# Loading q and k of the first four groups four tokens to a partition, one half of the heads on each partition half

## The chip, the cores and the metric

The kernel runs on one core of one Trainium2 chip. The metric is the device time of one execution in microseconds, the median of the timed runs. A profiled execution gives the span, the engines' records and the granted TensorE clock. A run is called slow when it is over 1.5% above the fastest of the same kernel.

## The reference

Attention over 4 batches, 8 heads, 768 tokens and 64 channels per head, with 4 sink tokens and a window of 128, then a feed-forward layer (512 to 2048, exact GELU, 2048 to 512) on all 3072 tokens.

```python
scores = scale * np.matmul(q, k.transpose(0, 1, 3, 2))
keep = is_sink | in_window                 # rel = query - key in 0..127, or key < 4
scores = np.where(keep, scores, -1e9)
a = softmax(scores)
attn = np.matmul(a, v)
x = attn.transpose(0, 2, 1, 3).reshape(B * S, H * D)
h = x @ w_in
g = 0.5 * h * (1.0 + erf(h / np.sqrt(2)))
out = g @ w_out                            # float32
```

The inputs q, k and v are 0.1 times normal numbers, so the scores are close to zero and the softmax is nearly flat. The comparison does not vouch for the order of q and k.

## The kernel before

The tokens are cut into twelve groups of 256. Everything that the first 60 us need comes through one load queue in a fixed order, into ten staging buffers:

```python
STREAM = [
    ("q", 0), ("k", 0), ("v", 0), ("q", 1), ("k", 1), ("wi", 0), ("wi", 1), ("v", 1), ("wi", 2),
    ("wi", 3), ("wi", 4), ("wi", 5), ("wi", 6), ("wi", 7), ("k", 2), ("wo", 1), ("q", 2),
    ("wo", 2), ("wo", 0), ("v", 2), ("q", 3), ("wo", 3), ("k", 3), ("wo", 4), ("wo", 5),
    ("wo", 6), ("wo", 7), ("v", 3),
]
# then q, k, v of groups 4 to 11
```

`wi` and `wo` are eighths of the two weight matrices. Each item is 512 KB. "q3" below means the q of group 3, and so on. A load of q or k has two tokens to a partition, 128 partitions, 512 bytes in one piece:

```python
def pump(limit=None):
    ...
        st = stage.tile([P, 1024], FP32, name="st", tag="st")
        if kind in SRC:
            ...
            nc.sync.dma_start(
                out=st[:, 0:w].rearrange("p (h c) -> p h c", c=2 * D),
                in_=src.rearrange("h (p r) d -> p h (r d)", r=2),
            )
```

`take` casts an item to bf16 on the engines that a hand-made list of operations names. Then q and k are transposed on TensorE, and one or two engines copy the result out of PSUM:

```python
def qk_transpose(g, w, *engs, pt=None, pairs=(0, NPAIR)):
    ...
    for p in range(*pairs):
        for r in range(2):
            nc.tensor.transpose(
                pt[:, :, p, r * HP : (r + 1) * HP] if w else pt[:, r, p, :],
                ..., ident)
    ...
    for o, eng in enumerate(engs or (nc.vector,)):
        ps = slice(pairs[0] + o * n, pairs[0] + (o + 1) * n)
        copy(eng, dst[:, :, ps], pt[:, :, ps])
```

Scores, exponentials, masks and output products of groups 0 to 3 are woven with the products of the feed-forward layer. From about 60 us on, groups 4 to 11 run in a steady pattern that the change does not touch.

The softmax here doesn't subtract the row's maximum and nothing guards it: scores larger than these inputs give would overflow.

Of the kernel before, what the change touches and what calls it, by code (L numbers as in the profile page):

```python
# [12 lines left out]
BF16 = mybir.dt.bfloat16  # L13
# [61 lines left out]
def kernel(  # L75
# [11 lines left out]
    nc = tc.nc  # L87
    P = nc.NUM_PARTITIONS

    B, H, S, D = q.shape  # L90
# [11 lines left out]
    NPAIR = H // 2  # L102
    NKT = DM // P
    NFT = DFF // P
    NBP = S // (2 * P)
# [130 lines left out]
    def pump(limit=None):  # L236

        while head[0] < (limit or len(stream)):
            n = head[0]
            if n >= NST and not freed[n - NST]:  # L240
                return
            kind, j, *half = stream[n]
            st = stage.tile([P, 1024], FP32, name="st", tag="st")
            if kind in SRC:
                b, i = divmod(j, NBP)
                hs = slice(half[0] * H // 2, (half[0] + 1) * H // 2) if half else slice(0, H)
                src = SRC[kind][b, hs, i * Q2 : (i + 1) * Q2, :]
                w = src.shape[0] * 2 * D
                nc.sync.dma_start(  # L249
                    out=st[:, 0:w].rearrange("p (h c) -> p h c", c=2 * D),  # L250
                    in_=src.rearrange("h (p r) d -> p h (r d)", r=2),
                )
            elif kind == "wi":
                nc.sync.dma_start(  # L254
                    out=st.rearrange("p (t f) -> p t f", f=FW),
                    in_=moe_w_in[:, ts(j // 2, FW)].rearrange("(t p) f -> p t f", p=P)[
                        :, 2 * (j % 2) : 2 * (j % 2) + 2, :
                    ],
                )
            else:  # L260
                nc.sync.dma_start(
                    out=st.rearrange("p (f c) -> p f c", c=DM),
                    in_=moe_w_out[j * NW * P : (j + 1) * NW * P, :].rearrange(
                        "(f p) c -> p f c", p=P
                    ),
                )
            staged[stream[n]] = st
            head[0] += 1
# [6 lines left out]

    def take(item, *engs):

        kind, j, *half = item
        st = staged.pop(item)
        eng = engs[0]  # L280
        if kind == "wi":
# [15 lines left out]
                        src[HP * e : HP * (e + 1), r, :, :],  # L297
                    )
        else:

            n = NPAIR // 2 if half else NPAIR
            o = half[0] * n if half else 0
            if (kind, j) not in cast:
                if kind == "q":
                    cast[kind, j] = c16p.tile([P, 2, H, D], BF16, name="q16")
                else:
                    cast[kind, j] = c16p.tile([P, NPAIR, 2, 2, D], BF16, name="k16")
            t = cast[kind, j]
            if kind == "q":
                dst = t[:, :, 2 * o : 2 * (o + n), :].rearrange("p r h d -> p h r d")  # L310
                src = st[:, 0 : n * 4 * D].rearrange("p (h r d) -> p h r d", r=2, d=D)
            else:
                dst = t[:, o : o + n].rearrange("p a r h d -> p a h r d")
                src = st[:, 0 : n * 4 * D].rearrange("p (a h r d) -> p a h r d", h=2, r=2, d=D)
            n = dst.shape[1] // len(engs)
            for o, eng in enumerate(engs):
                copy(eng, dst[:, o * n : (o + 1) * n], src[:, o * n : (o + 1) * n])
# [36 lines left out]
        QKT["k", g] = qktp.tile([P, 2, NPAIR, 2, HP], BF16, name="kt")  # L354
        return QKT["k", g]

    def qk_transpose(g, w, *engs, pt=None, pairs=(0, NPAIR)):


        src = cast["qk"[w], g]  # L360
        if pt is None:
            pt = psB.tile([P, 2, NPAIR, P], BF16, name="qkps", tag="bank")
        for p in range(*pairs):
            for r in range(2):
                nc.tensor.transpose(
                    pt[:, :, p, r * HP : (r + 1) * HP] if w else pt[:, r, p, :],
                    src[:, p, r, :, :].rearrange("s h d -> s (h d)") if w else src[:, r, 2 * p : 2 * p + 2, :].rearrange("s h d -> s (h d)"),
                    ident,
                )
        if ("qk"[w], g) not in QKT:  # L370
            (k_tile if w else q_tile)(g)
        dst = QKT["qk"[w], g].rearrange("k e p r s -> k e p (r s)") if w else QKT["qk"[w], g]
        n = (pairs[1] - pairs[0]) // max(1, len(engs))
        for o, eng in enumerate(engs or (nc.vector,)):
            ps = slice(pairs[0] + o * n, pairs[0] + (o + 1) * n)
            copy(eng, dst[:, :, ps], pt[:, :, ps])

    def big16():

# [24 lines left out]

    def warm_up(n, ps):

        for _ in range(n):
            nc.tensor.matmul(
                ps[:, 0:P], lhsT=ident, rhs=ident, start=True, stop=True, skip_group_check=True
            )  # L410

    ETS = {}

# [314 lines left out]
    def run(ops):  # L728

        pt = {}  # L730
        for op in ops:
# [5 lines left out]
            elif name == "take":  # L737
                take(tuple(args), *engs)
                pump(where["q", 6])
            elif name in ("T", "T2"):  # L740
                g, w = args[0:2]
                if name == "T2":
                    pt2 = psC.tile([P, 2, NPAIR, P], BF16, name="qkps2", tag="po2") if spare else None
                    qk_transpose(g, w, *engs, pt=pt2, pairs=(2 * args[2], 2 * args[2] + 2))
                elif len(args) > 2:
                    if g not in pt:
                        pt[g] = big16()
                    qk_transpose(g, w, *engs, pt=pt[g][:, w])
# [111 lines left out]
```

## Time and profile before

| | before |
|---|---|
| median (2 runs) | 226.98 us (226.87 to 227.09) |
| span of the profiled run | 224.7 us |
| TensorE busy | 214.5 us, 95% |
| mean granted clock | 0.999 |
| groups 0 to 3 end, second chunk's first feed-forward product starts | 59.4 us |

The page of the profile gives busy time by engine, the span in 40 slices, the queues, and the chain of work that ended last. The prediction below shows its main rows. In the views PE is TensorE, PEld its weight loads, DVE VectorE, ACT ScalarE, POOL GpSimd, and SP the engine whose queue issues the loads. First, TensorE's queue runs in order, so a wait of TensorE in the first 60 us is carried to the end unless a later wait takes it up. The row of the granted clock tells how fast TensorE may run in a slice (9 is full); before, it is 9 in all of them:

```profile
PEclk9999999999999999999999999999999999999999
```

"Landing" of a load below means the last of its sixteen completion increments in the trace.

### The profile page before, as it was taken

The page shows a single profiled execution, that of the slowest core. Times are in us where ns is not written, and L with a number is a line of the kernel's source. Part 1 is how long each engine was busy: PE and PEld are TensorE (multiplying, and loading weights), DVE is VectorE, ACT ScalarE, POOL GpSimd, SP SyncE. Part 2 cuts the span into 40 slices and gives each one's busy share as a digit, 9 for nine tenths or more (in the row PEclk, how much of TensorE's full clock was granted, in tenths as well). Part 3 has the DMA queues.
Part 4 walks back from the last instruction along what each step waited for, and adds up shares of the span by engine and source line. Part 5 has one row for each costly group of instructions (what it writes and reads, how often), then busy time and mean ns, then how long its engine had stood idle before and what let it go on. Part 6 is the DMA issues. An engine that isn't in the chain of part 4 may idle for free.

```text
span 224.7 us, 4333 instructions
## 1 busy us (share of the span) xinstructions
PE 214.5 (95%) x1742; PEld 118.4 (53%) x1762; DVE 111.0 (49%) x266; ACT 124.0 (55%) x154; POOL 51.9 (23%) x95
## 2 busy tenths in 40 slices
PE   7998999899999999999999999999999999999993
PEld 7665887455544465444455444455444465444452
DVE  4378304997690288480197580297550397100121
ACT  3677757955365974065973165963157972278000
POOL 8238726544220011320011400011400011300000
PEclk9999999999999999999999999999999999999999
DMA  6999999999396994477994487995582024500112
GB/s 168 291 351 386 344 340 325 371 284 308 118 186 112 305 282 100 96 144 148 300 250 99 93 167 166 293 217 106 107 170 39 0 51 100 126 10 0 47 47 93
DMA packets 70051, 40.12 MB, mean 179 GB/s; under 512 B 27152, under 2 KB 64272, under 8 KB 70032
## 3 DMA queue, kind: packets, MB, share of 16 engines
q1 hardware_dynamic: 67968, 34.48, 59.5%
q0 software_dynamic: 1920, 5.25, 9.6%
q8 instruction: 13, 0.21, 0.4%
q10 hardware_dynamic: 144, 0.13, 0.2%
q14 instruction: 6, 0.05, 0.1%
HBM read 27.26 MB, written 6.29 MB: 149 GB/s over the span
## 4 chain that ended last, share of the span: by engine, by line
PE 82%; DVE 4%; DMA 4%; SPq 4%; issue 2%; ACT 1%; POOL 1%
PE po L670 34%; PE big L603 29%; PE bank L537 4%; DMA st<-in_v_dram 4%; PE big L467 4%; PE big L636 3%; SPq L249 3%; PE po L636 2%; PE bank L603 2%; PE bank L517 1%; POOL vo L274 1%; SPq L254 1%; ACT et L476 1%; DVE et L484 1%; PE bank L578 1%
## 5 line engine op out<-in xcount | busy, mean ns | idle before, releaser
L670 PE MATMUL po<-WOUT,gt 128*128 128x512 bf16 (+1 forms) x380 | 86.5, 371 | 2.0 <-issue 1.6
L603 PE MATMUL big<-xt,WIN 128*128 128x512 bf16 x300 | 66.1, 379 | 0.2
L670 PEld LDWEIGHTS <-gt 128*128 128x128 bf16 x400 | 36.1, 98 | 39.1 <-issue 3.7
L622 ACT ACTIVATE gt<-big 128x1024 bf16<-128x1024 f32 (+1 forms) x32 | 30.6, 969 | 44.7 <-PE big L603 44.7
L603 PEld LDWEIGHTS <-WIN 128*128 128x128 bf16 x320 | 31.3, 98 | 37.8
L476 ACT ACTIVATE et<-big 128x1024 bf16<-128x1024 f32 (+1 forms) x48 | 43.6, 952 | 10.7 <-PE big L467 10.5
L685 POOL DMA_DIRECT2D out_dram<-osb x40 | 22.9, 578 | 111.2 <-DVE rz L555 79.8
L484 DVE TENSOR_TENSOR et<-et,mask 128x1024 bf16<-128x1024 bf16 x30 | 21.8, 731 | 32.6 <-ACT et L476 32.0
L274 DVE COPY osb<-po 128x512 f32<-128x512 f32 (+1 forms) x24 | 15.9, 665 | 37.8 <-PE po L670 29.5
L559 DVE TENSOR_TENSOR xg<-bank,rz 128x256 bf16<-128x256 f32 x44 | 18.7, 424 | 1.5
L537 PEld LDWEIGHTS <-et 128*128 128x128 bf16 x352 | 14.8, 97 | 6.6 <-issue 1.2
L274 DVE CAST vo<-st 64x512 bf16<-64x512 f32 x38 | 16.9, 443 | 1.8 <-DMA st<-in_v_dram 1.4
L467 PE MATMUL big<-qt,kt 64*128 64x128 bf16 (+1 forms) x256 | 15.6, 238 | 0.5 <-DVE kt L274 0.2
L616 ACT ACTIVATE gt<-big 128x1024 bf16<-128x1024 f32 (+1 forms) x8 | 9.8, 1238 | 11.0 <-PE big L603 11.0
L537 PE MATMUL bank<-vo,et 128*128 128x65 bf16 x326 | 14.9, 193 | 0.1
L636 PEld LDWEIGHTS <-WIN 128*128 128x128 bf16 x128 | 12.2, 98 | 1.6 <-issue 0.2
L491 DVE TENSOR_TENSOR et<-et,mask 128x768 bf16<-128x768 bf16 x14 | 7.8, 564 | 9.9 <-ACT et L476 9.5
L467 PEld LDWEIGHTS <-kt 64*128 64x128 bf16 x256 | 8.4, 94 | 7.9 <-issue 5.3
L701 ACT ACT_TABLE_LOAD x9 | 11.5, 1283 | 0.2
L555 DVE RECIPROCAL rz<-bank 128x4 f32<-128x4 f32 x44 | 7.7, 174 | 6.4 <-PE bank L537 3.9
L274 DVE CAST q<-st 128x1024 bf16<-128x1024 f32 (+1 forms) x12 | 7.6, 634 | 6.0 <-DMA st<-in_q_dram 5.8
L636 PE MATMUL big<-xt,WIN 128*128 128x256 bf16 x80 | 10.4, 272 | 0.0
(83 smaller groups left out, 146.8 us busy)
## 6 DMA issues: line engine op xcount, KB each, us to landing
st<-in_q_dram SPq DMA_DIRECT2D x12, 512.0 KB, 7.0
st<-in_k_dram SPq DMA_DIRECT2D x12, 512.0 KB, 6.7
st<-in_v_dram SPq DMA_DIRECT2D x12, 512.0 KB, 7.8
out_dram<-osb POOLq DMA_DIRECT2D x40, 128.0 KB, 2.8
st<-in_moe_w_in_dram SPq DMA_DIRECT2D x8, 512.0 KB, 9.7
st<-in_moe_w_out_dram SPq DMA_DIRECT2D x8, 512.0 KB, 8.0
out_dram<-osb SPq DMA_DIRECT2D x3, 256.0 KB, 2.0
kt<-k SPq DMA_TRANSPOSE x16, 2.8
```

The costliest lines, as they stand in the source:

```text
L274: eng.tensor_copy(out=out, in_=in_)
L467: nc.tensor.matmul(ps[:, hl, c : c + n * P], lhsT=kt(gk, p, ek, rows), rhs=qt(g, p, e, n, rows), start=not add, stop=True, skip_group_chec ...
L476: nc.scalar.activation(out=et[:, :, c0:], in_=ps[:, :, c0:], func=AF.Exp, scale=att_scale)
L484: nc.vector.tensor_tensor(out=et.rearrange("p h (e n) -> p (h e) n", e=2), in0=et.rearrange("p h (e n) -> p (h e) n", e=2), in1=mask.unsqu ...
L537: nc.tensor.matmul(pos[n][:, e * PV + hl * DV : e * PV + (hl + 1) * DV], lhsT=ets[n][:, hl, c : c + P], rhs=vo[:, h, :], start=e == 0 and ...
L559: nc.vector.tensor_tensor(out=XG[g][:, :, 2 * p : 2 * p + 2, :], in0=po[:, 0 : 2 * PV].rearrange("p (e h c) -> p e h c", e=2, h=2)[:, :, : ...
L603: nc.tensor.matmul(outs[a], lhsT=WIN[:, t, ts(f, P)], rhs=XT[c][:, :, t, :], start=(t == 0), stop=(t == NKT - 1),)
L622: nc.scalar.activation(out=gt.rearrange("k a n -> k (a n)"), in_=src, func=AF.Gelu)
L636: nc.tensor.matmul(out4[a], lhsT=WIN[:, t, ts(f, P)], rhs=XT[c][:, 2 * half : 2 * half + 2, t, :], start=(t == 0), stop=(t == NKT - 1), sk ...
L670: nc.tensor.matmul(po, lhsT=GT[c, f // 4][:, f % 4, ts(m, P)], rhs=WOUT[:, f, cols], start=(f == 0), stop=(f == NFT - 1),)
L685: nc.gpsimd.dma_start(out=out[r0 : r0 + P, :].rearrange("(s r) c -> r s c", r=2)[r], in_=osb[HP * r : HP * (r + 1), :],)
L701: nc.scalar.activation(out=warm[:, 1:2], in_=warm[:, 0:1], func=func)
```

## The change

The intent is longer packets: 1024 bytes instead of 512 for q and k of the first 1024 tokens. Four tokens go to one partition, so 256 tokens fill 64 partitions; heads 0 to 3 go to the lower half of the partitions and heads 4 to 7 to the upper half. One load becomes two of 256 KB. The transposed tokens then stand in another order in PSUM, and the copy out of PSUM puts them right by reading pairs that are 32 elements apart.

```diff
-            if kind in SRC:
+            if kind in "qk" and j < 4:
                 b, i = divmod(j, NBP)
+                for hg in range(2):
+                    nc.sync.dma_start(
+                        out=st[HP * hg : HP * (hg + 1), :].rearrange("p (h c) -> p h c", c=4 * D),
+                        in_=SRC[kind][
+                            b, hg * H // 2 : (hg + 1) * H // 2, i * Q2 : (i + 1) * Q2, :
+                        ].rearrange("h (p r) d -> p h (r d)", r=4),
+                    )
... (casts: the same elements in another order)
-        for p in range(*pairs):
-            for r in range(2):
+        for j in range(2):
+            for a in range(2):
+                for r in range(2):
+                    if w:
+                        dst = pt.rearrange("k e (g j) (r a n) -> k j r a g e n", j=2, r=2, a=2)
+                    else:
+                        dst = pt.rearrange("k r (g j) (e a n) -> k j r a g e n", j=2, e=2, a=2)
+                    nc.tensor.transpose(dst[:, j, r, a], ..., ident)
...
-            copy(eng, dst[:, :, ps], pt[:, :, ps])
+            copy(
+                eng,
+                dst[:, :, ps].rearrange("k b p (c n a) -> k b (p c) n a", c=2, a=2),
+                pt[:, :, ps].rearrange("k b p (c a n) -> k b (p c) n a", c=2, a=2),
+            )
... (warm_up: the same columns of fill matmuls, in instructions of up to 512)
```

More of the change, by code (lines that the diff above doesn't have):

```diff
@@ L241, in pump @@
                 return
-            kind, j, *half = stream[n]
+            kind, j = stream[n]
             st = stage.tile([P, 1024], FP32, name="st", tag="st")
-            if kind in SRC:
+            if kind in "qk" and j < 4:
                 b, i = divmod(j, NBP)
-                hs = slice(half[0] * H // 2, (half[0] + 1) * H // 2) if half else slice(0, H)
-                src = SRC[kind][b, hs, i * Q2 : (i + 1) * Q2, :]
-                w = src.shape[0] * 2 * D
+                for hg in range(2):
[5 more added lines that the diff above has]
+                    )
+            elif kind in SRC:
+                b, i = divmod(j, NBP)
                 nc.sync.dma_start(
-                    out=st[:, 0:w].rearrange("p (h c) -> p h c", c=2 * D),
-                    in_=src.rearrange("h (p r) d -> p h (r d)", r=2),
+                    out=st.rearrange("p (h c) -> p h c", c=2 * D),
+                    in_=SRC[kind][b, :, i * Q2 : (i + 1) * Q2, :].rearrange(
+                        "h (p r) d -> p h (r d)", r=2
+                    ),
                 )
@@ L276, in take @@
     def take(item, *engs):
-        kind, j, *half = item
+        kind, j = item
         st = staged.pop(item)
@@ L299, in take @@
         else:
-            n = NPAIR // 2 if half else NPAIR
-            o = half[0] * n if half else 0
-            if (kind, j) not in cast:
-                if kind == "q":
-                    cast[kind, j] = c16p.tile([P, 2, H, D], BF16, name="q16")
-                else:
-                    cast[kind, j] = c16p.tile([P, NPAIR, 2, 2, D], BF16, name="k16")
-            t = cast[kind, j]
-            if kind == "q":
-                dst = t[:, :, 2 * o : 2 * (o + n), :].rearrange("p r h d -> p h r d")
-                src = st[:, 0 : n * 4 * D].rearrange("p (h r d) -> p h r d", r=2, d=D)
-            else:
-                dst = t[:, o : o + n].rearrange("p a r h d -> p a h r d")
-                src = st[:, 0 : n * 4 * D].rearrange("p (a h r d) -> p a h r d", h=2, r=2, d=D)
+            if j < 4:
+                t = c16p.tile([P, 2, 4, 2, D], BF16, name=kind + "16")
+                dst = t.rearrange("p a r h d -> p a h r d")
+                src = st.rearrange("p (a h r d) -> p a h r d", h=2, r=4, d=D)
+            elif kind == "q":
+                t = c16p.tile([P, 2, H, D], BF16, name="q16")
+                dst = t.rearrange("p r h d -> p h r d")
+                src = st.rearrange("p (h r d) -> p h r d", r=2, d=D)
+            else:
+                t = c16p.tile([P, NPAIR, 2, 2, D], BF16, name="k16")
+                dst = t.rearrange("p a r h d -> p a h r d")
+                src = st.rearrange("p (a h r d) -> p a h r d", h=2, r=2, d=D)
+            cast[kind, j] = t
             n = dst.shape[1] // len(engs)
@@ L355, in k_tile, with qk_transpose @@
         return QKT["k", g]
-    def qk_transpose(g, w, *engs, pt=None, pairs=(0, NPAIR)):
+    def qk_transpose(g, w, *engs, pt=None):
         src = cast["qk"[w], g]
@@ L362, in qk_transpose @@
             pt = psB.tile([P, 2, NPAIR, P], BF16, name="qkps", tag="bank")
-        for p in range(*pairs):
-            for r in range(2):
-                nc.tensor.transpose(
-                    pt[:, :, p, r * HP : (r + 1) * HP] if w else pt[:, r, p, :],
-                    src[:, p, r, :, :].rearrange("s h d -> s (h d)") if w else src[:, r, 2 * p : 2 * p + 2, :].rearrange("s h d -> s (h d)"),
-                    ident,
-                )
-        if ("qk"[w], g) not in QKT:
-            (k_tile if w else q_tile)(g)
-        dst = QKT["qk"[w], g].rearrange("k e p r s -> k e p (r s)") if w else QKT["qk"[w], g]
-        n = (pairs[1] - pairs[0]) // max(1, len(engs))
-        for o, eng in enumerate(engs or (nc.vector,)):
-            ps = slice(pairs[0] + o * n, pairs[0] + (o + 1) * n)
-            copy(eng, dst[:, :, ps], pt[:, :, ps])
+        for j in range(2):
[5 more added lines that the diff above has]
+                        dst = pt.rearrange("k r (g j) (e a n) -> k j r a g e n", j=2, e=2, a=2)
+                    nc.tensor.transpose(
+                        dst[:, j, r, a],
+                        src[:, j, 2 * a + r].rearrange("s h d -> s (h d)"),
+                        ident,
+                    )
+        (k_tile if w else q_tile)(g)
+        dst = QKT["qk"[w], g].rearrange("k e p r s -> k e p (r s)") if w else QKT["qk"[w], g]
+        n = NPAIR // len(engs)
+        for o, eng in enumerate(engs):
+            ps = slice(o * n, (o + 1) * n)
+            copy(
+                eng,
+                dst[:, :, ps].rearrange("k b p (c n a) -> k b (p c) n a", c=2, a=2),
+                pt[:, :, ps].rearrange("k b p (c a n) -> k b (p c) n a", c=2, a=2),
+            )
     def big16():
@@ L405, in warm_up @@
     def warm_up(n, ps):
-        for _ in range(n):
+        while n > 0:
+            w = min(n, 4)
             nc.tensor.matmul(
-                ps[:, 0:P], lhsT=ident, rhs=ident, start=True, stop=True, skip_group_check=True
+                ps[:, 0 : w * P],
+                lhsT=ident,
+                rhs=ident.unsqueeze(1).to_broadcast((P, w, P)),
+                start=True,
+                stop=True,
+                skip_group_check=True,
             )
+            n -= w
     ETS = {}
@@ L739, in run @@
                 pump(where["q", 6])
-            elif name in ("T", "T2"):
+            elif name == "T":
                 g, w = args[0:2]
-                if name == "T2":
-                    pt2 = psC.tile([P, 2, NPAIR, P], BF16, name="qkps2", tag="po2") if spare else None
-                    qk_transpose(g, w, *engs, pt=pt2, pairs=(2 * args[2], 2 * args[2] + 2))
-                elif len(args) > 2:
+                if len(args) > 2:
                     if g not in pt:
```

## The prediction

> **What bounds the kernel now.** I read the page first: which engine is busy, and where it is not.
>
> ```profile
> span 224.7 us, 4333 instructions
> ...
> PE 214.5 (95%) x1742; PEld 118.4 (53%) x1762; DVE 111.0 (49%) x266; ACT 124.0 (55%) x154; POOL 51.9 (23%) x95
> ...
> PE   7998999899999999999999999999999999999993
> ...
> DMA  6999999999396994477994487995582024500112
> GB/s 168 291 351 386 344 340 325 371 284 308 118 186 112 305 282 100 96 144 148 300 250 99 93 167 166 293 217 106 107 170 39 0 51 100 126 10 0 47 47 93
> ```
>
> TensorE is busy 95% of the span. A slice is 5.6 us; slices below 9 lie in the first nine, about 50 us, and in the last. In those 50 us the DMA row stands at 9 and stays there until 58 us. So the end is set by TensorE, whose queue is in order: what is lost in the first 50 us shifts all that follows, and nothing later can win it back. The changed lines touch only this stretch (the first four groups of 256 tokens). About 10 us of TensorE idle is the most that a perfect repair could give, 4.5%; a stall of 4.5 us would be needed for a loss of 2%.
>
> Next the chain of work that ended last, in order of time, for the first 20 us: which wait ends last there?
>
> ```profile
> 1.94 1.36 SPq L249
> ...
> 3.35 1.62 SPq L249
> ...
> 5.00 1.74 SPq L249
> ...
> 9.08 9.11 DMA st<-in_v_dram
> ```
>
> Columns are start, length, what. The load queue is held up, 1.6 to 1.7 us for each 512 KB load, and the eighth load of the stream (v of group 1) lands at 18.19. GpSimd then casts it until 21.6, and the waits of TensorE show 1.0 us for that cast (at 21.70). From there TensorE runs closed up to 36 us. So the landing time of load 8 sets the start of all that follows; q0, k0, q1 and k1 lie in front of it.
>
> Rates by window (mean DMA share, then GB/s, stand last):
>
> ```profile
> 5.00:11.00 6.00, 5.52 (x75) 4.29 (x73) 2.44 (x5) 3.68 (x6) 2.20 (x6) 1.00 1.20 290
> 18.00:22.00 4.00, 3.01 (x43) 2.31 (x40) 3.12 (x7) 3.15 (x4) 3.53 (x5) 1.00 1.07 390
> ```
>
> From 5 to 11 us only q, k, v come, as 512-byte packets: 290 GB/s, 1.81 us for a load of 524288 bytes. From 18 to 22 us weights come as 2048-byte packets: 390 GB/s. The packet records give the same: 33.6 ns mean for 512 bytes, 88.6 ns for 2048. The intent of the change is plain: 1024-byte packets for q and k.
>
> A second critical place is at 37 to 47 us, where the chain passes through VectorE (0.69 us kt copy, then casts, L484, q copy), and the timeline of VectorE is closed:
>
> ```profile
> 37.64 0.69 DVE L274 COPY kt<-qkps 128x1024 bf16<-128x1024 bf16 x1 [0.19 <-PE qkps L365]
> 38.25 1.06 DVE L274 CAST WOUT<-st 128x1024 bf16<-128x1024 f32 x1
> 39.23 0.83 DVE L274 CAST q<-st 128x512 bf16<-128x512 f32 x1
> ...
> 41.56 0.69 DVE L484 TENSOR_TENSOR et<-et,mask 128x1024 bf16<-128x1024 bf16 x1
> 42.17 1.26 DVE L274 CAST k<-st 128x512 bf16<-128x512 f32 x1
> 43.35 0.68 DVE L274 COPY qt<-qkps 128x1024 bf16<-128x1024 bf16 x1
> ```
>
> No idle bracket after the second line until 44.95; TensorE waits for L484 at 42.3 and for L559 at 44.63 (0.66 us).
>
> **What the Trainium skill says.** (1) "SBUF — State Buffer", section on the DMA port swizzle: partitions 0 to 63 reach only 8 of 16 ports, as do 64 to 127; it measured 196 GB/s for 64 partitions against 328 for 128 at 1 MiB, and two loads to the two halves do not add up. The trace has the like: output stores from 64 partitions against those from 128.
>
> ```profile
> out_dram<-osb POOLq DMA_DIRECT2D x40, 128.0 KB, 2.8
> ...
> out_dram<-osb SPq DMA_DIRECT2D x3, 256.0 KB, 2.0
> ```
>
> Half the bytes take longer. In the packet records a pair of half stores (2 x 128 KB, about 188 us) takes 1.59 us, 165 GB/s, and one full 256 KB store (212.6 us) 0.80 us, 327 GB/s. The agreement is good, though queue and direction differ from a load. (2) "VectorE: DVE Perf Modes", auto-detection: two 16-bit elements per cycle out of PSUM need step 1. The trace agrees for contiguous copies: 0.68 us for 1024 elements, under the 1.07 us that one per cycle at the 0.96 GHz of that page would need. (3) "DMA: Bandwidth & Descriptors", rules: two transfers to disjoint halves serialize.
>
> **The change, part by part.**
> Loads. Each of 8 loads (512 KB, 1024 packets of 512 bytes over 128 partitions) becomes two of 256 KB, 256 packets of 1024 bytes each, on 64 partitions. The effective time of a packet is 16 engines x bytes / rate: 28.2 ns at 512 and 84 ns at 2048; a straight line between gives 46.8 ns at 1024, 350 GB/s, 1.50 us a load. That is the hoped case: 0.31 us saved on each, 1.2 us over the four loads ahead of v1. With half the ports, an estimate from the SBUF page's 8 x 27.2 GB/s is 218 GB/s, 2.41 us: 0.60 us lost on each, 2.4 us over four. The upper bound from this trace is half of 390, 195 GB/s, 2.69 us: 3.5 us over four. I choose 2.4. Group 1's k then lands near 14.9 instead of 12.4, the weights and v1 likewise 2.4 later (20.6), its cast ends near 24.0. v1 remains what TensorE waits for, so its whole stream shifts 2.4 us. The next four loads lose 2.4 more, but q2's cast is over at 32.2 and TensorE takes it at 36.1; only k3 (cast from 42.2, needed for the copy at 45.4) could cost about 0.5.
>
> Copies out of PSUM. The eight copies now read pairs 32 elements apart. On VectorE the two-per-cycle mode should go: 512 cycles more at 0.96 GHz, 0.53 us for 1024 elements, 0.27 for 512. VectorE has four full ones (q1, q2, k2, q3) and three halves: 2.9 us in all. The early ones hide under the wait for v1. In the stretch of 37 to 47 us, q2 and k2 delay the chain to L484 by up to 1.0, q3's another 0.5: I put 1.2 on the path. ScalarE copies (1.01 and 0.59 us) I leave unchanged, having no view of a strided one.
>
> Casts: same elements, same runs of 64, no change. Transposes: the same 64, output runs 64 bytes long; q with runs of 128 elements and k with runs of 64 both take 219 ns now, so no change. Warm-up: 102 fill matmuls of 128 columns become 27 of mostly 512, the same columns; 12 fills now take 0.83 us, 69 ns each, so some 0.1 us per group, in a stretch that waits for loads: 0.
>
> Sum: 227.0 + 2.4 + 1.2 + 0.5, less 1.3 because some of these overlap each other and existing idle (0.66 us at 44.6): 229.8.
>
> **The rivals.** A: packets win. The two halves follow each other on the same engines; should those get out of step, some serve one half while others serve the other, and all ports work. Then v1 lands 1.2 us earlier, but TensorE reached that wait only 1.0 us before, and slower copies take 0.3 of it early and 1.2 later: 226 to 227.5. For it: 512-byte packets visibly cost; against it: the half stores at 165 GB/s, two in a row. B: loads are slow and everything is on the path: 3.5 for v1, 1.5 VectorE, 1 for k3 and the late weights: 233, over 2%. C: VectorE's copies stay fast and loads half-hidden: 228.5. D: everything hidden: 227; against it stands that the wait at 21.70 leaves no slack for a later landing.
>
> **Range and chances.** Half the ports or something near: 65%, giving 230.5 give or take 1; the packets win or cancel: 35%, 227.2 give or take 0.7. Together 229.8 with 226.5 to 232.0 as the range. Over 2% slower means above 231.5: 0.17. Over 2% faster means below 222.4, more than the early idle can give by this change: 0.01. Within: 0.82.
>
> **What would show it.** Rate in the early q and k windows: near 218 or below (right), near 350 (wrong, rival A). Landing of v1: near 20.6 against 18.2, and TensorE's wait for that cast still there near 24. VectorE copies from PSUM: 1.2 us for 1024 elements, 0.68 if I am wrong. TensorE's stretch of 36 to 48 us longer by about 1 us with waits on VectorE. After 60 us nothing should differ but the shift. What would make it wrong: engines that share out the ports well, or TensorE bound so tightly to other waits that the shift is absorbed.

## The result

| | before | after |
|---|---|---|
| median (2 runs each) | 226.98 us | 235.24 us (235.19 to 235.28) |
| ratio of the fast runs | | 1.0364, 95% interval 1.0319 to 1.0408 |
| span of the profiled run | 224.7 us | 233.6 us |
| mean granted clock | 0.999 | 0.985 |

The changed kernel is 3.6% slower, and its time is above the predicted range. Ratios in this document are the mean time of one kernel's fast runs over the mean of the other's of the same rounds, so they are not quite the ratios of the medians quoted.

The page of the changed kernel, rows that answer to those of before (busy time, TensorE and its clock by slices of 5.84 us, GB/s, loads of q and k):

```profile
span 233.6 us, 4207 instructions
...
PE 217.9 (93%) x1668; PEld 114.9 (49%) x1688; DVE 114.2 (49%) x266; ACT 123.9 (53%) x154; POOL 52.1 (22%) x95
...
PE   7688899859999999999999999999999999999993
...
PEclk9799999979999999999999999999999999999999
...
GB/s 136 237 295 365 310 240 295 249 351 220 274 187 170 112 274 290 104 90 174 147 299 209 120 108 151 232 290 114 146 133 92 3 45 94 90 45 3 45 45 91
...
st<-in_q_dram SPq DMA_DIRECT2D x8, 256.0 KB, 8.8
st<-in_k_dram SPq DMA_DIRECT2D x8, 256.0 KB, 9.7
```

The reader should see three things. The eight q and k items are now sixteen loads of 256 KB. TensorE has a hole in the ninth slice (5 tenths, 46.7 to 52.6 us), which it did not have before. The clock shows a 7 in the second and ninth slices, each where TensorE has been waiting.

The lag grows in two places. These are the shifts of the same instruction in the two traces:

| TensorE or ScalarE reaches | before, us | after, us | shift |
|---|---|---|---|
| first exponential | 9.34 | 12.89 | +3.56 |
| transposes of q2 | 36.00 | 40.20 | +4.20 |
| first output product of group 2 | 41.98 | 47.50 | +5.52 |
| transposes of k3 | 44.70 | 53.24 | +8.54 |
| first feed-forward product after group 3 | 59.42 | 68.26 | +8.84 |
| end | 225.03 | 233.86 | +8.83 |

So the lag is 3.6 us by the first exponential, grows by 4.3 more between 40 and 53 us, and does not grow after 60 us. These are lags at a point, not losses that add up: two runs described below come to the transposes of q2 1.3 us earlier (after_exact) and 3.4 us later (two_queues) than the changed kernel, and neither time differs from its time clearly. In the changed kernel the late place sets the end.

**The early place.** The changed kernel's chain of work that ended last (start, length, what):

```profile
3.57 7.08 DMA st<-in_v_dram
...
11.87 0.70 DVE kt L284
12.62 0.23 PE big L493 x2
```

The third and fourth of the first scores (L493) wait for VectorE's share of the copy of k, and that copy stands in VectorE's queue behind the cast of v0, whose load landed at 10.65 (8.68 before). Before, the first scores started at 8.95 and did not wait for VectorE at all.

**The late place.** First the chain of the kernel before, where wo3's cast had been waiting in VectorE's queue for its turn, not for its load:

```profile
40.06 0.59 DVE WOUT L274
...
41.56 0.69 DVE et L484
```

Then the same piece of the changed kernel's chain:

```profile
36.84 10.78 DMA st<-in_moe_w_out_dram
47.64 0.93 DVE WOUT L284
...
49.50 0.70 DVE et L510
50.25 0.40 PE bank L563 x4
```

And its VectorE timeline (start, busy time, what, in brackets the idle time ahead and what ended it):

```profile
42.09 1.21 DVE L284 COPY kt<-qkps 128x1024 bf16<-128x1024 bf16 x1
...
45.90 0.43 DVE L284 CAST q<-st 128x512 bf16<-128x512 f32 x1 [1.99 <-DMA st<-in_q_dram]
47.64 0.93 DVE L284 CAST WOUT<-st 128x1024 bf16<-128x1024 f32 x1 [1.32 <-DMA st<-in_moe_w_out_dram]
```

Before, wo3 landed at 38.85 and its cast came at 40.06, so it had 1.21 us to spare. Now it lands at 47.62, 8.77 later, and the cast follows at once. VectorE's queue is in order: behind that cast stand v2's casts and the mask (L510, before L484) that the output products of group 2 need. The mask is 7.94 later: 8.77, less the 1.21 to spare, plus 0.38 of longer queue. So a mask that has nothing to do with the weights is held up because the in-order engine ahead of it waits for a load of weights.

By stretches (start and end, length, busy time of PE, PEld, DVE, ACT and POOL, then clock, DMA share, GB/s):

```profile
5.00:11.00 6.00, 4.13 (x26) 2.05 (x24) 1.19 (x3) 2.64 (x4) 0.70 (x5) 0.85 1.12 235
...
48.00:50.00 2.00, 0.00 (x0) 0.00 (x0) 1.92 (x4) 0.00 (x0) 0.03 (x1) 1.00 1.04 364
50.00:52.00 2.00, 1.53 (x11) 0.97 (x13) 1.95 (x5) 1.54 (x2) 0.66 (x1) 0.53 1.07 365
```

From 5 to 11 us 235 GB/s move instead of 290. From 48 to 50 us TensorE does nothing, and after it the granted clock is 0.53.

### The profile page after: what moved, and what is told of

Same layout as the page of the kernel before. It is cut to its first block, busy times and chain, and to the rows that moved or that the text cites. A ratio compares the mean times of both kernels' runs of the same rounds, so it can differ in the third digit from the quotient of the medians.

```text
span 233.6 us, 4207 instructions
## 1 busy us (share of the span) xinstructions
PE 217.9 (93%) x1668; PEld 114.9 (49%) x1688; DVE 114.2 (49%) x266; ACT 123.9 (53%) x154; POOL 52.1 (22%) x95
## 4 chain that ended last, share of the span: by engine, by line
PE 77%; DMA 8%; DVE 7%; ACT 3%; issue 2%; SPq 2%; ACTq 0%
PE po L696 32%; PE big L629 28%; DMA st<-in_moe_w_out_dram 5%; PE bank L563 4%; PE big L493 4%; DMA st<-in_v_dram 3%; PE big L662 2%; ACT et L502 2%; PE bank L629 2%; DVE et L510 2%; SPq L249 2%; PE bank L543 1%; DVE vo L284 1%; DVE kt L284 1%; DVE et L517 1%
## 5 line engine op out<-in xcount | busy, mean ns | idle before, releaser
L510 DVE TENSOR_TENSOR et<-et,mask 128x1024 bf16<-128x1024 bf16 x30 | 22.0, 740 | 32.6 <-ACT et L502 32.0
L493 PE MATMUL big<-qt,kt 64*128 64x128 bf16 (+1 forms) x256 | 16.3, 241 | 1.4 <-DVE kt L284 1.0
L493 PEld LDWEIGHTS <-kt 64*128 64x128 bf16 x256 | 8.7, 95 | 10.3 <-issue 7.3
```

The costliest lines, as they stand in the source:

```text
L493: nc.tensor.matmul(ps[:, hl, c : c + n * P], lhsT=kt(gk, p, ek, rows), rhs=qt(g, p, e, n, rows), start=not add, stop=True, skip_group_chec ...
L510: nc.vector.tensor_tensor(out=et.rearrange("p h (e n) -> p (h e) n", e=2), in0=et.rearrange("p h (e n) -> p (h e) n", e=2), in1=mask.unsqu ...
```

## The experiments

The theory: the loads are the whole loss, since a load to half of the partitions is slow. A first rival: the strided copies on VectorE lengthen its closed stretches and make the waits. A second: the number of loads, sixteen instead of eight, is what costs. A third: the lowered clock is a cause. Three further questions came up on the way: why the late loads cost more than the early ones, why a fast form of the loads gains nothing, and what a false wait in the copies is worth.

All kernels of a call ran on one chip with the kernel before: 226.54, 226.56, 226.62 and 226.53 us median in the four calls (7 runs each). Every other kernel has 4 runs. The table gives all of them; the texts follow. The edits are shown shortened; conditions that confine them to q and k of the groups named are left out.

| run | median, us | range | ratio to before, 95% interval |
|---|---|---|---|
| half_ports | 236.54 | 234.72 to 236.9 | 1.0398 [1.0343, 1.0454] |
| by_heads | 227.36 | 226.28 to 228.5 | 1.0021 [0.9974, 1.0069] |
| copies_only | 229.34 | 228.58 to 231.23 | 1.012 [1.006, 1.018] |
| stripes | 231.93 | 230.55 to 233.62 | 1.0225 [1.0164, 1.0286] |
| groups_0_1 | 228.66 | 228.43 to 229.84 | 1.010 [1.007, 1.013] |
| groups_2_3 | 232.39 | 232.09 to 233.26 | 1.026 [1.0236, 1.0285] |
| stripes_plain | 227.17 | 226.61 to 227.92 | 1.0016 [0.9991, 1.004] |
| stripes_v_first | 231.32 | 230.29 to 231.74 | 1.020 [1.0171, 1.0229] |
| copies_exact | 227.10 | 226.84 to 227.34 | 1.002 [1.0002, 1.0038] |
| fills | 234.63 | 233.83 to 234.97 | 1.0347 [1.0321, 1.0373] |
| two_queues | 235.06 | 234.12 to 235.45 | 1.0365 [1.0331, 1.0398] |
| stripes_exact | 232.41 | 229.57 to 233.56 | 1.0212 [1.0145, 1.028] |
| group_3 | 229.78 | 229.45 to 230.62 | 1.0155 [1.0128, 1.0181] |
| adjacent_full | 229.45 | 228.47 to 230.37 | 1.0128 [1.0091, 1.0166] |
| adjacent_half | 232.45 | 231.33 to 233.0 | 1.0255 [1.0225, 1.0286] |
| after_exact | 235.44 | 233.99 to 236.48 | 1.0389 [1.0346, 1.0433] |

### half_ports: the kernel before, each q and k load in two partition halves

```diff
+ for g2 in range(2):
+     rows = slice(HP * g2, HP * (g2 + 1))
      nc.sync.dma_start(
-         out=st[:, 0:w]..., in_=src.rearrange("h (p r) d -> p h (r d)", r=2))
+         out=st[rows, 0:w]..., in_=src.rearrange("h (p r) d -> p h (r d)", r=2)[rows])
```

> The kernel before; each of the eight q and k loads of groups 0 to 3 is split into two loads by partition half (rows 0 to 63, then 64 to 127), still 512-byte packets, same places, same copies. Result correct. Theory 1 (loads that reach one partition half run at about half the rate, 225 GB/s in the changed kernel's first 14 us against 290): v of group 1 has its last packet near 18.9 us as in the changed kernel (16.3 before), the last v load near 53.9 (46.2 before), and the time rises by most of the 8.3 us: 232 to 235 us. Theory 2 (the strided copies out of PSUM carry the loss): 227 to 228.5 us.

Measured: 236.54 us, 1.5 above the range of theory 1. Packets stay at 512 bytes, transposes and copies are those of before, and the whole loss is there. Stretches of its trace, same columns:

```profile
44.00:46.00 2.00, 1.26 (x11) 0.37 (x9) 0.00 (x0) 0.95 (x3) 0.00 (x0) 1.00 1.18 192
46.00:48.00 2.00, 0.74 (x10) 0.47 (x11) 0.43 (x1) 0.38 (x1) 1.24 (x2) 1.00 1.19 184
```

The queue is busy (DMA share 1.18 and 1.19) and moves 192 and 184 GB/s, while TensorE is busy for 2.00 of the four us and VectorE for 0.43. The copies fall as the main cause.

### by_heads: the same number of loads, all partitions

```diff
+ for g2 in range(2):
+     hh = slice(g2 * H // 2, (g2 + 1) * H // 2)
-     out=st..., in_=src...
+     out=st...[:, hh], in_=src...[:, hh]
```

> Control of the number of loads: the kernel before with each of the same eight loads split into two by heads, each over all 128 partitions, 512-byte packets. Result correct. Theory 1 (partition halves): no change, 226.5 to 227.5 us. Rival (more and smaller loads cost by themselves): several us, up to 8.

Measured: 227.36 us, a ratio whose interval holds 1 and ends at 1.0069, or 1.6 us. So the number of loads is not the main cost; the second rival falls. One side effect is of use below: k0 lands at 8.47 instead of 6.86 although all partitions are used.

### copies_only: the changed kernel with the loads of before

Its output is wrong, which doesn't matter for the time.

```diff
-            if kind in "qk" and j < 4:
+            if False:
```

> The changed kernel with its q and k loads put back to one full load of 512-byte packets each; casts, transposes, strided copies and wide warm-up stay. The order of tokens and heads is wrong on purpose, so the result is wrong; times are valid. Theory 1: the copies (0.53 us more each on VectorE for 1024 elements, as the trace shows) cost 1 to 1.5 us: 227.5 to 229 us. Theory 2 (copies carry the loss): above 231 us.

Measured: 229.34 us, 2.8 over before and a little above the first theory's range. The TensorE timeline says where most of it begins:

```profile
8.86 0.28 PE L493 MATMUL big<-qt,kt 64*128 64x256 bf16 x2
10.57 0.23 PE L493 MATMUL big<-qt,kt 64*128 64x128 bf16 x2 [1.42 <-DVE kt L284]
```

The third and fourth of the first scores wait 1.42 us for VectorE. They read head pair 0, which ScalarE has copied; VectorE copies pairs 2 and 3. In the trace these matmuls wait for VectorE's semaphore. Each engine's copy writes its pairs in both 128-token blocks, which fits a tracking that takes this region for one unbroken stretch, from its first pair in block 0 to its last in block 1; the next experiment tests whether the two blocks matter. The wait guards nothing, and VectorE's copy stands behind v0's cast.

That the two parts interleave is not enough, though. The kernel before shares the copy of k in the same way, pairs 0 and 1 to ScalarE and 2 and 3 to VectorE, each in both blocks, and its four first scores run ahead of VectorE's part:

```profile
8.31 0.59 ACT L272 COPY kt<-qkps 128x512 bf16<-128x512 bf16 x1
8.96 0.34 PE L467 MATMUL big<-qt,kt 64*128 64x256 bf16 x4
9.91 0.42 DVE L274 COPY kt<-qkps 128x512 bf16<-128x512 bf16 x1
```

What is new is the longer pattern in which the same region is written. Why that brings the wait is not shown.

### copies_exact: each shared copy written block by block

As copies_only.

```diff
-            copy(eng, dst[:, :, ps]..., pt[:, :, ps]...)
+            for e in range(2):      # where two engines share the copy
+                copy(eng, dst[:, e, ps]..., pt[:, e, ps]...)
```

> The kernel with the full 512-byte loads and the strided copies (order wrong on purpose), with each copy that two engines share written as two instructions, one for each block of 128 tokens. In the kernel without this the first scores of pair 0 wait for VectorE's half of k (pairs 2 and 3), which they do not read, 1.42 us at 10.6 us, behind the cast of v; now they wait for ScalarE's half alone. If that wait is a cost of its own: the first exponential starts near 9.4 us in place of 10.8, and 228.0 to 228.8 us in place of 229.3. If the strided copies at 37 to 48 us carry all of it: 229 to 229.6 us.

Measured: 227.10 us, below what either side expected. In its timeline the same scores run in one group (the form of this kernel has the scores at L501):

```profile
8.81 0.35 PE L501 MATMUL big<-qt,kt 64*128 64x256 bf16 x4
```

So the false wait was about 2.2 us of the 2.8 (the two runs are of different calls), and the strided reads, with everything else in that kernel, cost 0.5.

### groups_0_1 and groups_2_3: the change in two groups at a time

```diff
-            if kind in "qk" and j < 4:
+            if kind in "qk" and j in NEW:      # (0, 1) or (2, 3); else as before
```

> The changed kernel with its new loads, casts, transposes and copies in groups 0 and 1 alone (tokens 0 to 511); groups 2 and 3 as before. Result correct. Theory A (the loads ahead of v of group 1 cost some 4 us, as in the changed kernel at 22 us, and the later four cost the other 4): 229.5 to 232 us. Theory B (a delay of the early part is absorbed by the waits of 36 to 48 us, so that the later loads carry nearly all): 227 to 229 us.

> The changed kernel with its new form in groups 2 and 3 alone; groups 0 and 1 as before, so v of group 1 has its last packet near 16.3 us. Result correct. Theory A: 229.5 to 232 us, and the two halves together give the 8.3 us. Theory B: 233 to 235 us.

Measured: 228.66 and 232.39 us, +2.1 and +5.8. The sum, 7.9, is about the whole loss of 8.3, so the two add up. Neither theory has both times in its ranges. What was missed is that the late two groups cost nearly three times as much as the early two. The landing of v3, the last load of this stretch, shows the same: 47.73 before, 50.29 with groups 0 and 1, 53.92 with groups 2 and 3. A split load costs 0.64 us in the early groups (2.56 over four) and 1.55 in the late ones (6.19 over four).

### group_3, adjacent_full, adjacent_half: why a late load costs more

group_3 is the change in q3 and k3 alone. The other two move the late loads: q3 and k3 come directly behind k2 and q2. adjacent_full has the loads of before, adjacent_half the changed form in groups 2 and 3.

```diff
-    ("wi", 7), ("k", 2), ("wo", 1), ("q", 2), ("wo", 2), ("wo", 0), ("v", 2), ("q", 3), ("wo", 3), ("k", 3), ...
+    ("wi", 7), ("k", 2), ("q", 2), ("q", 3), ("k", 3), ("wo", 1), ("wo", 2), ("wo", 0), ("v", 2), ("wo", 3), ...
```

> The changed kernel's loads, transposes and copies in group 3 alone (q3, k3); all else as before. What is to be read first is the landing of the last load of weights and v before 60 us, 47.73 us before, 50.29 with groups 0 and 1 (four split loads, 0.64 us each), 53.92 with groups 2 and 3 (1.55 us each). Theory M (a half load costs more when it stands between loads of weights, each one by itself): two split loads land the last v near 47.73 + 2 x 1.55 = 50.8. Theory N (the first two half loads throw the sixteen DMA engines out of step, and only a series of them costs 1.5): about 47.73 + 2 x 0.6 = 49.0. Time: M 229.5 to 231, N 227.5 to 229.

> The kernel before with its late loads in another order: k2, q2, q3, k3 stand next to each other, ahead of wo1, wo2, wo0, v2, wo3; full loads. It is the reference for the next run. The sum of the loads is the same, so the last weights (wo6) should land where they did before, 44.65 us give or take 0.5; the time may be a little longer because wo1, wo2, wo0 come 3.5 us later: 227 to 229.

> The same order with the four loads of groups 2 and 3 in the changed form (1024-byte packets, one half of the partitions each). Theory M (a half load is dear because loads of weights stand on both sides of it): next to each other only the ends mix, so four cost 0.6 to 0.8 us each and wo6 lands 2.4 to 3.2 us later than in adjacent_full; early, groups 0 and 1 have cost 0.64 each like this. Rival: the price in this stretch is 1.55 each in any order (something of the later stretch itself, as its deep queue): wo6 lands 6.2 us later than in adjacent_full. Time: M +2 to +3.5 us over adjacent_full, rival +5 to +6.

Landings in us:

| load | before | groups_2_3 | group_3 | adjacent_full | adjacent_half |
|---|---|---|---|---|---|
| wi7 | 26.33 | 28.02 | 26.20 | 26.57 | 27.95 |
| k3 | 40.57 | 47.29 | 44.43 | 33.05 | 36.69 |
| wo6 | 44.65 | 51.12 | 48.21 | 45.17 | 47.71 |
| v3 | 47.73 | 53.92 | 51.39 | 48.28 | 50.84 |

Two split loads among loads of weights (group_3) cost 3.66 us at v3, 1.83 each; theory M expected 50.8 and got 51.39, theory N's 49.0 is out. (Each landing is of one profiled run; v3 lands from 47.73 to 48.06 in before, copies_only and copies_exact, which have the same loads.) Four that stand together cost 2.54 at wo6, 0.64 each, the price of the early groups. So the late stretch as such is not dear. A split load is dear when full loads stand on both sides of it. The records of single packets fit: from 27 to 47 us the 2048-byte packets of the weights take 91 ns each on average before, and 126 ns in the changed kernel, beside half loads. Why full loads slow so much beside half ones is not shown by any run. The times followed as M said: adjacent_half is 3.0 us over adjacent_full. The order itself costs 2.9 us, since the weights come later, so the repair gains nothing: 232.45 against 232.39 for groups_2_3.

### two_queues: the upper halves of groups 0 and 1 from ScalarE's queue

```diff
-                    nc.sync.dma_start(
+                    (nc.scalar if hg and j < 2 else nc.sync).dma_start(
```

> The changed kernel with the upper-half loads of q and k of groups 0 and 1 issued from ScalarE's queue in place of the sync engine's, so that both halves can be in flight together. Result correct. If the halves then use all ports: 300 GB/s or more in the first q and k loads, k of group 0 landed near 7 us in place of 8.3, and 231 to 234 us. If loads to the two halves do not add up even so: 225 GB/s and 235 to 236 us.

Measured: 235.06 us. From 5 to 11 us the trace shows 236 GB/s against 235 in the changed kernel. Two halves on two queues do not add up to the full rate, as the Trainium skill has it in "SBUF — State Buffer", the section on two transfers to the two halves (+6% there). The run shows one thing more. v0 now lands at 12.82 instead of 10.65, the first exponential comes at 15.12 instead of 12.89 and the transposes of q2 3.4 us later than in the changed kernel, yet the time is the same: wo3 lands at 47.79 against 47.62, and TensorE waits for it.

### fills: the clock held up

```diff
-    ("T", [0,0], "A"), ("T", [0,1], "AV"), ... ("av", [2,0], "")
+    ("T", [0,0], "A"), ("warm", [28], ""), ("T", [0,1], "AV"), ... ("av", [2,0], "W44")
```

> The changed kernel with matmuls whose results nothing reads put into TensorE's two long waits: 28 blocks of 128 columns before the transposes of k of group 0, 44 before the first output product of group 2. Result correct. If the lowered clock behind those waits (granted 0.50 to 0.86 at 10 to 14 us and 0.53 to 0.62 at 50 to 54 us) is a loss by itself: the clock stays at 1.00 and the time falls by 1.5 to 3 us, to 232.5 to 233.7 us. If the slow clock only fills time in which TensorE would wait anyway: 234.5 to 235.5 us.

Measured: 234.63 us, 0.6 under the changed kernel's median, and the granted clock of the span is 1.000 instead of 0.985:

```profile
50.00:52.00 2.00, 1.95 (x22) 1.01 (x21) 2.00 (x4) 1.54 (x2) 0.47 (x1) 1.00 1.04 311
```

The clock there is 1.00 instead of 0.53, and the time hardly moves: the intervals of the two ratios overlap, so even the 0.6 us is not clear of the noise. The third rival falls as a main cause; the low clock is above all a mark of the wait. The Trainium skill, "TensorE: Matmul & The Clock Gate", says in its table of the two states that the clock falls after an idle window of about 3.4 us; here it stood at 0.53 after TensorE had been idle for 2.5 us at a stretch, by the bracket of its timeline:

```profile
50.25 0.40 PE L563 MATMUL bank<-vo,et 128*128 128x65 bf16 x4 [2.51 <-DVE et L510]
```

This line is of the changed kernel; the page's figure and this wait differ, and the wait is what was measured.

### after_exact: the changed kernel without the false wait

The edit is that of copies_exact, on the changed kernel itself; the order is right.

> The changed kernel with each shared copy written in two pieces, one for each 128-token block, so that the first scores no longer wait for the part of VectorE that they do not read. Theory: the change is bound by its loads, above all those of 27 to 50 us, and the false wait lies beside them: 234.6 to 235.5, no difference of over 0.6 us, though the first exponential comes about 1 us earlier. Rival: the 2.2 us that this form was worth with full loads are on the path here too: 233.0.

Measured: 235.44 us, as the theory said. The first exponential comes at 11.03 instead of 12.89, and the transposes of q2 at 38.86 instead of 40.20. Then the transposes of q3 come at 46.36 instead of 46.38: the lead has gone, because there both kernels wait for loads that land at the same time (q3 at 45.79 and 45.80). The false wait, worth 2.2 us with full loads, is worth nothing here.

### stripes: long packets and all partitions

The two loads go to the even and to the odd partitions instead of the lower and upper half. A permuted identity in the transposes puts the tokens back; by construction the order is that of the change.

```diff
-    out=st[HP * hg : HP * (hg + 1), :]...
+    out=st.rearrange("(s g) c -> s g c", g=2)[:, hg]...
...
-                        ident,
+                        perm,      # ident with its columns "(s g)" in the order "(g s)"
```

> The changed kernel with one difference: the two loads of a tile go to the even and to the odd partitions in place of the lower and the upper half, and the transposes use a permuted identity to undo that. Same bytes, packets of 1024 bytes, number of loads and copies; result correct. Theory 1: the rate goes to 330 to 360 GB/s in the first q and k loads, v of group 1 has its last packet near 15.2 us, and the time falls to 226.5 to 229 us (copies remain). If 64 partitions as such or 1024-byte packets were slow: still 233 to 235 us.

Measured: 231.93 us, between the two ranges. The loads do what the change wanted: from 5 to 13 us the 1024-byte packets take 48 ns on average, against 78 ns in the changed kernel, and from 5 to 11 us 314 GB/s move, against 235. The best stretch of its trace:

```profile
8.00:10.00 2.00, 1.75 (x15) 0.84 (x14) 0.47 (x2) 1.41 (x3) 0.38 (x1) 1.00 1.09 361
```

v3 lands at 46.73, 1.0 us earlier than before. And yet the kernel is 2.25% slower. TensorE is 2.0 us late at the transposes of q2 and 5.3 at those of k3. VectorE's timeline, then GpSimd's, in the late stretch:

```profile
41.60 1.26 DVE L289 CAST q<-st 128x512 bf16<-128x512 f32 x1
42.78 1.52 DVE L289 CAST WOUT<-st 128x1024 bf16<-128x1024 f32 x1
44.34 2.32 DVE L289 CAST vo<-st 64x512 bf16<-64x512 f32 x2
```

```profile
41.16 5.22 POOL L289 CAST WOUT<-st 128x1024 bf16<-128x1024 f32 x4 [2.35 <-DMA st<-in_moe_w_out_dram]
```

Where GpSimd is idle, the same three forms of cast take 0.43, 0.68 and 0.86 us (in the changed kernel's timeline at 50.20, there a cast of k, at 43.22 and at 48.60). Here GpSimd casts four weights without a gap from 41.16, because they have landed early, and VectorE has come late; the two meet. The Trainium skill, "SBUF — State Buffer", section "Who interferes with whom", says that VectorE in a two-port mode and GpSimd share a pair of ports and shut each other out; the stretched casts agree. They are 3.1 us longer in all, about what TensorE loses between the two transposes, so the meeting fits as the cause of that; no run takes it away alone.

### stripes_plain and stripes_v_first

stripes_plain is stripes with contiguous copies out of PSUM. Its output is wrong, which doesn't matter for the time. stripes_v_first is stripes with v3 loaded ahead of the last four weights.

```diff
- copy(eng, dst[:, :, ps].rearrange(...), pt[:, :, ps].rearrange(...))
+ copy(eng, dst[:, :, ps], pt[:, :, ps])
```

```diff
- ("k", 3), ("wo", 4), ("wo", 5), ("wo", 6), ("wo", 7), ("v", 3),
+ ("k", 3), ("v", 3), ("wo", 4), ("wo", 5), ("wo", 6), ("wo", 7),
```

> The kernel with loads to even and odd partitions, and with its copies out of PSUM made contiguous, so the order of tokens is wrong and so is the result, on purpose. If the strided copies alone make the rest of its loss: 226 to 227.5 us, the gain of the fast loads. If the earlier landing of the last weights, whose casts then hold GpSimd from 41.2 to 46.4 us without a gap and stretch VectorE's casts (q 0.42 to 1.26, weights 0.68 to 1.52, v 0.86 to 2.32 us), is a loss by itself: 228 to 231 us.

> The kernel with loads to even and odd partitions, with v of group 3 loaded ahead of the last four pieces of the second weights in place of behind them, so that these land some 1.7 us later, about when they land before the change. Same traffic, same instructions; result correct. If the collision of the casts on GpSimd and VectorE is what it loses beside the copies: 228 to 230 us, and the VectorE casts at 41 to 46 us short again (0.42, 0.68, 0.86). If not: 231 to 233 us as without it.

stripes_plain: 227.17 us. With fast loads and with nothing in the copies to pay for, there is no gain over before. One reason can be read: k0, split, lands at 8.33 in stripes_plain and at 6.86 before, and v3, at the end of the stretch, at 47.56 against 47.73: the faster packets have not brought earlier landings, so what earlier landings would be worth is not tested. stripes_v_first: 231.32 us, where 228 to 230 was expected if the meeting of the casts was the loss. This was a miss; v2's casts still took 1.60 us and the mask behind them 1.45 instead of 0.69, so shifting the last weights alone does not undo the meeting of the two engines, and whether the meeting is the loss stays open.

### stripes_exact

The edit of copies_exact, on stripes.

> The kernel with loads to even and odd partitions, with the shared copies written per block of 128 tokens as well. Same order of tokens restored, result correct. The best form of the change that I have: if the false wait on k's other half and the strided reads make up its loss, 229 to 230.5 us in place of 231.9; if the loss is in the collision of casts at 41 to 47 us, 231 to 232.5 us.

Its four runs go from 229.57 to 233.56 us. The slowest of them, the profiled one, was slow, so its trace is not compared; the three fast runs give the ratio of 1.0212, and it does not beat before. The time is in the range expected if the meeting of the casts is the loss. Why the block-wise copies did not help here as they did with full loads stays open. No version beats the kernel before.

## Why the prediction was wrong, point by point

- **Half the ports: right.** I put 218 GB/s on the early windows, and 235 came; two loads to the two halves follow each other. half_ports, stripes and two_queues bear it out from three sides.
- **0.60 us lost on each load: right in the early four, and mis-sized in the late four.** This is the term that failed. It measured 0.64 in groups 0 and 1 and 1.55 in groups 2 and 3, because there each split load has full loads of weights around it (group_3 1.83, adjacent_half 0.64). The prediction had 4.8 us on the last loads; the changed kernel has v3 9.33 later.
- **"q2's cast is over at 32.2 and TensorE takes it at 36.1; only k3 ... could cost about 0.5": the second failed step.** The slack of q2 was real: in groups_2_3 its load lands 3.7 us later than before and its transposes start 0.3 later. But I looked at q2 and k3 alone. wo3 had 1.2 us of slack and q3 about 1.8, and both stand in VectorE's queue ahead of the mask. Of the 8.5 us that TensorE lags at the transposes of k3, 7.9 are that mask's lag; I had put 0.5 and a share of the copies on this stretch.
- **"v1 remains what TensorE waits for, so its whole stream shifts 2.4 us": wrong.** v1 landed 1.34 us later than in the trace before, and the stream had already shifted by 3.56 at the first exponential. The wait had moved to the front: k0's landing (+1.46) and the false wait behind v0's cast. The reading of the kernel before was weak too. groups_2_3 has its early loads, yet there v1 landed at 16.68 instead of 18.19, and the transposes of q2 came no earlier (36.40 against 36.11 in TensorE's timeline): TensorE waited 1.3 us for a cast of weights on GpSimd instead. So v1's landing alone did not set the stream. What the load queue lost is as predicted: wi5 lands at 26.04 instead of 23.57, 2.47 later.
- **"What is lost in the first 50 us shifts all that follows": not so.** A lead of 1.3 us (after_exact) and a lag of 3.4 us (two_queues) against the changed kernel at the transposes of q2 are gone at those of k3, which start at 53.10 and 52.93 against 53.34 in TensorE's timeline: all three have waited for the late loads.
- **Copies out of PSUM: right in size, wrong on the path.** VectorE took 1.22 us for 1024 elements, where I had said 1.2, so the two-per-cycle mode is gone, as the Trainium skill would have it in "VectorE: DVE Perf Modes", section on auto-detection; ScalarE's copies stayed at 1.0 us. But I put 1.2 us of this on the path, and copies_exact shows about 0.5 (0.0 to 0.9 by its interval). What did cost, 2.2 us in copies_only, was a dependency that no view of the kernel before could show. In the change itself it lay beside the loads (after_exact).
- **Transposes, casts and warm-up as no cost: no run contradicts it.** copies_exact has all three and is 0.2% over before.
- **After 60 us nothing but the shift: right**, +8.84 there and +8.83 at the end.
- **The rivals.** A (the packets win) is out: the halves stay slow, and in stripes_plain even fast packets gained nothing, though there the landings came no earlier. B was right that the loads are slow and that k3 and the late weights count, but its 233 put 1 us on these. I gave slower by over 2% a chance of 0.17; groups_0_1 alone, +2.1 us, is about what I had priced. C (fast copies) is out by the 1.22 us, D (everything hidden) by the time.
- **The sum.** The two branches as weighted (0.65 x 230.5 + 0.35 x 227.2) give 229.3, not 229.8; the miss is not there.

What stays open: why full loads slow beside half ones, what brings the false wait, and whether the meeting of the casts is the loss in stripes and stripes_exact.

## What to carry to other kernels

Keep a load on all partitions before making its packets longer: here twice the packet length on half of the partitions moved 235 GB/s where 290 had been, and the loads of weights between them slowed as well. When a queue is behind, follow every load to the in-order engine that takes it, and ask what else stands behind that cast; the load that hurts may belong to data that the waiting work does not use. When two engines share a copy and the form of its pattern changes, look in the trace for a wait on the engine whose part is not read; here writing each part block by block took it away.

## What the Trainium skill lacked or had wrong

- "SBUF — State Buffer", on the port swizzle: it tells what half of the partitions costs in a single transfer, and not what it does to full ones beside it. Here a pair of half loads cost 0.64 us more than one full load among its like, and 1.55 to 1.83 us between full loads of weights, whose packets took 126 ns on average instead of 91.
- "SBUF — State Buffer", the section on two transfers to the two halves: it says that only one transfer over all 128 partitions reaches all ports. Loads to every second partition, 64 each, moved 314 GB/s from 5 to 11 us and 361 from 8 to 10, where loads to the lower and upper halves moved 235, so 64 partitions are no such limit when they are spread over both halves.
- "DMA: Bandwidth & Descriptors": the rules do not say what splitting a load costs the first waiter. The second item, k0, landed at 8.47 us instead of 6.86 when q and k were each loaded in two parts over all partitions.
- "TensorE: Matmul & The Clock Gate": a lowered clock (0.53 behind a 2.5 us wait) reads like a cause. It had fallen after less idle time at a stretch than the page's window of about 3.4 us, and holding it at 1.00 with fill matmuls brought 0.6 us of 8.3, which is not clear of the noise.
- No page has it: when two engines share a copy, a reader can be made to wait for the engine whose part it does not read; 2.2 us in copies_only, gone in copies_exact.
